# Two B loads of block 2 issued from GpSimd, and C of pairs 4 and 5 scaled ahead of their B

## The chip, the core and the metric

The kernel runs on one NeuronCore of a Trainium2 chip. The metric is the device time of one execution in microseconds (us). A core has five engines with a program each: TensorE (PE; its weight loads are shown as PEld), VectorE (DVE), ScalarE (ACT), GpSimd (POOL) and SyncE (SP). They wait for one another by semaphores. Loads and stores are issued by SyncE, ScalarE or GpSimd and carried out by 16 DMA engines.

## The reference

Two layers are computed one after the other. The first is a state-space recurrence in chunks (batch 4, 8 heads, 768 tokens, head size 32, state size 16):

```
cum = cumsum(log a) within the chunk;  L[i,j] = exp(cum[i]-cum[j]) for i >= j, else 0
y[i] = sum_j (C[i].B[j]) L[i,j] x[j]  +  (C[i].state) exp(cum[i])
state = exp(sum log a) state + sum_j B[j] x[j] exp(cum[last]-cum[j])
```

Its result, seen as 3072 tokens of 256 values, goes through a bilinear layer with d_ff = 1536: `out = ((y @ w_a) * (y @ w_b)) @ w_out`. Inputs and output are float32; the matrix products run on float16 operands.

## The kernel before

**Tiling.** The 768 tokens are cut into six blocks of 128. Blocks 0 and 1 and blocks 2 to 5 take somewhat different paths; the change is about block 2, the first that goes all the way by the later path. A *pair* is half of a block's scores: pairs 4 and 5 are heads 0 to 3 and heads 4 to 7 of block 2, each over all four batches. Decay is put on the operands: C is multiplied by running products of `a`, B by their inverses, so that the scores C.B need only the causal mask afterwards.

**The way of a pair from block 1 on.**
- *Loads.* `load_q` (L160) loads a block's C and B with eight DMAs of 64 KB, one for each of C and B and each batch, into two tiles, cq and bq (32 partitions for a batch). `ALL_Q` (L158) gives the order: C of batches 0 to 3, then B of batches 0 to 3. A tile thus serves both pairs of a block, and a pair needs all four batches. From block 2 on `loads_b` (L711) loads B of a pair a second time, by token, into bn, for the state sums; `loads_x` (L729) loads x from GpSimd.
- *Scaling.* `scale_q` (L341; the instruction is at L346) multiplies cq by FC, or bq by FB, into one of three float16 planes (pair 4 has plane 1, pair 5 plane 2), on GpSimd. FB is made by a reciprocal on VectorE (L309).
- *Turning.* `turn` (L353, instruction L359) transposes C and B of a plane with one VectorE instruction.
- *Scores.* `scores` (L398, L404): the matmuls of a pair (16 from block 2 on) into four PSUM banks.
- *Masks.* `mask` (L442): of the four score tiles of pairs 4 and 5, three on VectorE (L449); the fourth is copied out of PSUM by ScalarE (L446, into tmp) and masked by GpSimd (L447).
- *Output of a block.* `outputs` (L532): matmuls with the state (L536) and of scores and x (L473 or L485), the state sums (L501 or L512, from bn scaled into bm by GpSimd at L333), and ScalarE's copy into XB (L558). `state_spread` and `state_decay` (L576, L586) carry the state on, on GpSimd.

**The second layer.** `bunit` (L659) makes one of twelve k slices of a block: two matmuls for x @ w_a (aps), two for x @ w_b (bps, both L667), ScalarE's copy asb (L612), VectorE's product hkb (L679). `bout` (L685) multiplies with w_out (L693); ScalarE evacuates (L705), and the result is stored. Blocks 0 and 1 are stored later, from a list. The second layer of one block fills TensorE while the other engines prepare the pairs of the next.

**What sets the order.** It is written out by hand: the lines from L774 on are run with a manual schedule, and each engine executes its instructions in the order of these lines. A load is an instruction in the program of the engine that issues it. SyncE's and ScalarE's loads share eight completion semaphores in turn, and a load waits until the earlier one with its semaphore has landed; GpSimd's loads have eight of their own. Around the change:
- SyncE: x of pairs 2 and 3 (L819, four DMAs), B of pair 3 (L820, two), then block 2's eight loads (L888), bn of pairs 4 and 5 (L889), block 3's eight (L932), bn of pairs 6 and 7 (L941).
- GpSimd: C of pairs 2 and 3, B of pairs 2 and 3 (L871 to L874), Ge (L877), `spread(0)` with spair and gV (L883), the masks of pairs 2 and 3 (L899, L901, L913), bm of pairs 2 and 3 (L914, L915), causal_q (L916, L917), then C and B of pair 4 and C and B of pair 5 (L933, L934), x of pair 4 (L935), bm of pairs 4 and 5 (L940).
- VectorE: k slices 0 and 1 of block 1 (L946), turning of pair 4 (L947), slices 2 and 3 (L948). TensorE: the matmuls of these four slices, then the scores of pair 4 (L949).

Of the kernel before, what the change touches and what calls it, by code (L numbers as in the profile page):

```python
# [28 lines left out]
def kernel(  # L29
# [13 lines left out]
    nc = tc.nc  # L43
# [114 lines left out]
    ALL_Q = tuple((w, b) for w in (1, 0) for b in range(nb))  # L158

    def load_q(eng, blk, parts=ALL_Q):  # L160
        if blk not in by_batch:
            by_batch[blk] = [inq.tile([128, H, 4, N], f32, name=n_, tag=n_) for n_ in ("bq", "cq")]
        return [
            eng.dma_start(
                by_batch[blk][w][32 * b : 32 * b + 32].rearrange("i h s n -> i h (s n)"),
                (B, C)[w][b, :, blk * Q : (blk + 1) * Q, :].rearrange("h (i s) n -> i h (s n)", s=4),
            )
            for w, b in parts
        ]

    def load2(eng, p, which):
        if p < P2:
            return [load1(eng, p, which, bt) for bt in range(2)]
        blk, bp = divmod(p, NBP)
        src = (B, C, x)[which][2 * bp : 2 * bp + 2, :, blk * Q : (blk + 1) * Q, :]
        return [
            eng.dma_start(  # L177
                by_token(pair_in[p][which]).rearrange("p t h n -> p (t h) n"), src.rearrange("t h q n -> q (t h) n")
            )
        ]  # L180
# [160 lines left out]
    def scale_q(p, which, eng):  # L341
        blk, u = divmod(p, NBP)
        f = (FB, FC)[which][:, blk - PJ // NBP, :, 4 * u : 4 * u + 4].rearrange("p s j -> p j s")
        plane, step = planes[p % NR], (48, N)[which]
        c0 = (0, 192)[which]
        eng.tensor_tensor(  # L346
            out=plane[:, c0 : c0 + 4 * step].rearrange("p (j c) s -> p j s c", c=step)[:, :, :, 0:N],
            in0=by_batch[blk][which][:, 4 * u : 4 * u + 4],
            in1=f.unsqueeze(3).broadcast_to((128, 4, 4, N)),
            op=ALU.mult,  # L350
        )
# [359 lines left out]
    def loads_b(*ps):  # L711
        for p in ps:
            if p < NP:
                tiles(p)
                load2(nc.sync, p, 0)

    def loads_q(blk):
        if blk < NBLK:
            load_q(nc.sync, blk)
# [9 lines left out]
    def loads_x(p):  # L729
        if p < NP:  # L730
            load2(nc.gpsimd, p, 2)
# [5 lines left out]
    def prep(p):  # L737
        if p < NP:
            scale_q(p, 1, nc.gpsimd)
            scale_q(p, 0, nc.gpsimd)  # L740
# [144 lines left out]
    aps = [unit_mm(p, k2, Wa) for p, k2 in late]  # L885
    asb = [evac_a(a_ps) for a_ps in aps]
    load2(nc.scalar, 2, 0)
    load_q(nc.sync, 2)  # L888
    loads_b(4, 5)  # L889
    for (p, k2), a_sb_ in zip(late, asb):  # L890
        times(p, k2, unit_mm(p, k2, Wb), a_sb_)
# [36 lines left out]
    for c in range(3):  # L928
        p, bt = divmod(c, NBP)
        out_mm(p, bt, o[c], range(6, NK))  # L930
        out_store(p, bt, o[c])
    loads_q(3)  # L932
    prep(4)  # L933
    prep(5)  # L934
    loads_x(4)  # L935
    outputs(1)
    state_sums(1)
# [128 lines left out]
```

## Time and profile before

| | |
|---|---|
| time, three runs | median 123.27 us (122.97 to 123.49) |
| the profiled execution | 123.0 us, of which the span of the trace is 121.2 us |
| TensorE busy | 115.5 us, 95% of the span |
| VectorE, ScalarE, GpSimd busy | 90.1, 67.3 and 57.4 us |
| moved by DMA | 12.13 MB in 59777 packets |

The profile is that of one execution. A line of a timeline gives start and length in us from the start of the span, the engine, the line of the kernel, the operation, the tiles written and read, partitions x elements, and how many; in brackets stands the idle time of the engine ahead of it, and what ended it, inferred from semaphores. Where a wait has several semaphores, the name given may be of one that was not last. L12 is line 12 of the kernel before. "q" behind an engine (SPq) means its instruction queue: a load's length there is that of the issue, not of the transfer. Queue q1 is SyncE's, q10 ScalarE's, q0 GpSimd's; kind "instruction" is program code. Ends of matmuls are modelled.

### The profile page before, as it was taken

The page shows a single profiled execution, that of the slowest core. Times are in us where ns is not written, and L with a number is a line of the kernel's source. Part 1 is how long each engine was busy: PE and PEld are TensorE (multiplying, and loading weights), DVE is VectorE, ACT ScalarE, POOL GpSimd, SP SyncE. Part 2 cuts the span into 40 slices and gives each one's busy share as a digit, 9 for nine tenths or more (in the row PEclk, how much of TensorE's full clock was granted, in tenths as well). Part 3 has the DMA queues.
Part 4 walks back from the last instruction along what each step waited for, and adds up shares of the span by engine and source line. Part 5 has one row for each costly group of instructions (what it writes and reads, how often), then busy time and mean ns, then how long its engine had stood idle before and what let it go on. Part 6 is the DMA issues. An engine that isn't in the chain of part 4 may idle for free.

```text
span 121.2 us, 3574 instructions
## 1 busy us (share of the span) xinstructions
PE 115.5 (95%) x1399; PEld 75.4 (62%) x1400; DVE 90.1 (74%) x165; ACT 67.3 (56%) x133; POOL 57.4 (47%) x90
## 2 busy tenths in 40 slices
PE   7989999999979999999999999999999999999990
PEld 5546799888524478644476464766465684645880
DVE  4998989979969995599966999677889436748000
ACT  0446666696647654677655737535645637575220
POOL 7994989679179999396902995200000000000000
PEclk9999999999999999999999999999999999999998
DMA  3999999994679999979992909112001111010132
GB/s 63 133 182 192 208 234 190 202 155 94 93 105 108 123 117 151 109 103 125 238 186 87 86 2 124 10 46 92 0 0 46 32 43 60 0 43 0 49 108 65
DMA packets 59777, 12.13 MB, mean 100 GB/s; under 512 B 54992, under 2 KB 59728, under 8 KB 59760
## 3 DMA queue, kind: packets, MB, share of 16 engines
q0 software_dynamic: 20256, 3.67, 37.6%
q1 hardware_dynamic: 35920, 7.74, 34.0%
q10 hardware_dynamic: 3584, 0.49, 2.6%
q8 instruction: 11, 0.18, 0.7%
q14 instruction: 6, 0.05, 0.1%
HBM read 12.42 MB, written 3.15 MB: 128 GB/s over the span
## 4 chain that ended last, share of the span: by engine, by line
PE 91%; DVE 4%; issue 1%; ACT 1%; POOL 1%; ACTq 0%
PE ops L693 22%; PE aps L667 21%; PE bps L667 20%; PE ops L637 5%; PE aps L598 5%; PE bps L598 4%; PE SC L404 4%; PE SC L238 3%; PE SC L473 2%; DVE t L449 1%; PE SC L536 1%; PE py L458 1%; POOL planes L346 1%; PE tc L238 1%; PE SC L485 1%
## 5 line engine op out<-in xcount | busy, mean ns | idle before, releaser
L612 ACT COPY asb<-aps 128x512 f32<-128x512 f32 x72 | 41.9, 586 | 16.9 <-PE aps L667 13.3
L679 DVE TENSOR_TENSOR hkb<-bps,asb 128x512 f16<-128x512 f32 x60 | 40.2, 685 | 11.9 <-ACT asb L612 10.3
L667 PE MATMUL aps<-XB,Wa 128*128 128x512 f16 x120 | 35.8, 379 | 0.0
L667 PE MATMUL bps<-XB,Wb 128*128 128x512 f16 x120 | 35.7, 379 | 0.0
L693 PE MATMUL ops<-Wo,hkb 128*128 128x256 f16 (+1 forms) x252 | 28.1, 268 | 0.0
L693 PEld LDWEIGHTS <-hkb 128*128 128x128 f16 x252 | 23.0, 98 | 3.8
L667 PEld LDWEIGHTS <-Wb 128*128 128x128 f16 x120 | 12.4, 103 | 13.5
L667 PEld LDWEIGHTS <-Wa 128*128 128x128 f16 x120 | 12.1, 103 | 11.5 <-issue 0.2
L449 DVE TENSOR_TENSOR t<-SC,causal_q 128x512 f16<-128x512 f32 x27 | 17.3, 680 | 2.4 <-PE SC L404 2.4
L705 ACT ACTIVATE osb<-ops 128x256 f32<-128x256 f32 (+1 forms) x20 | 7.6, 378 | 18.4 <-PE ops L693 18.4
L447 POOL TENSOR_TENSOR t<-tmp,causal_q 128x512 f16<-128x512 f32 x5 | 5.8, 1158 | 8.8 <-ACT tmp L446 8.8
L177 POOL DMA_DIRECT2D xn<-in_x_dram x8 | 9.5, 1191 | 0.0
L346 POOL TENSOR_TENSOR planes<-bq,FB 128x256 f16<-128x256 f32 x10 | 7.5, 768 | 3.5 <-DVE hkb L679 3.4
L449 DVE TENSOR_TENSOR t<-SC,causal 128x512 f16<-128x512 f32 x11 | 6.9, 681 | 1.2 <-PE SC L404 1.1
L346 POOL TENSOR_TENSOR planes<-cq,FC 128x256 f16<-128x256 f32 x10 | 7.5, 771 | 0.1
L446 ACT COPY tmp<-SC 128x512 f32<-128x512 f32 x10 | 5.8, 588 | 2.9 <-PE SC L404 2.5
L622 DVE TENSOR_TENSOR hk<-bps,asb 128x512 f16<-128x512 f32 x11 | 7.2, 671 | 0.2 <-ACT asb L612 0.2
L558 ACT ACTIVATE XB<-SC 128x512 f16<-128x512 f32 (+1 forms) x9 | 4.6, 548 | 4.1 <-PE SC L501 2.4
L598 PE MATMUL aps<-X2T,Wa 128*128 128x256 f16 x48 | 6.8, 273 | 0.0
L598 PE MATMUL bps<-X2T,Wb 128*128 128x256 f16 x48 | 6.6, 272 | 0.0
L447 POOL TENSOR_TENSOR t<-tmp,causal 128x512 f16<-128x512 f32 x5 | 5.7, 1155 | 1.7 <-ACT tmp L446 1.6
L359 DVE STREAM_TRANSPOSE turned<-planes 128x384 f32<-128x384 f32 x10 | 5.5, 562 | 1.0 <-POOL planes L346 1.0
(100 smaller groups left out, 109.0 us busy)
## 6 DMA issues: line engine op xcount, KB each, us to landing
out_dram<-osb SPq DMA_DIRECT2D x23, 128.0 KB, 1.9
cq<-in_C_dram SPq DMA_DIRECT2D x20, 64.0 KB, 3.5
bq<-in_B_dram SPq DMA_DIRECT2D x20, 64.0 KB, 3.5
bn<-in_B_dram SPq DMA_DIRECT2D x8, 128.0 KB, 4.3
xn<-in_x_dram POOLq DMA_DIRECT2D x8, 128.0 KB, 5.4
Wa<-in_moe_w_a_dram POOLq DMA_DIRECT2D x2, 384.0 KB, 7.2
Wb<-in_moe_w_b_dram POOLq DMA_DIRECT2D x2, 384.0 KB, 7.7
Wo<-in_moe_w_out_dram POOLq DMA_DIRECT2D x2, 384.0 KB, 6.6
```

Source lines behind the costliest of these rows:

```text
L177: eng.dma_start(by_token(pair_in[p][which]).rearrange("p t h n -> p (t h) n"), src.rearrange("t h q n -> q (t h) n"))
L346: eng.tensor_tensor(out=plane[:, c0 : c0 + 4 * step].rearrange("p (j c) s -> p j s c", c=step)[:, :, :, 0:N], in0=by_batch[blk][which][:, ...
L447: nc.gpsimd.tensor_tensor(out=o_, in0=tmp, in1=c_, op=ALU.mult)
L449: nc.vector.tensor_tensor(out=o_, in0=i_, in1=c_, op=ALU.mult)
L598: nc.tensor.matmul(ps[:, kk * 2 * Q : (kk + 1) * 2 * Q], W[k // 6][:, f, k % 6 // 3 * 384 : (k % 6 // 3 + 1) * 384].rearrange("p (c kk) -> ...
L612: (nc.vector.tensor_copy if on_dve else nc.scalar.copy)(asb, a_ps)
L622: eng.tensor_tensor(out=s["hk"][:, 2 * k2 : 2 * k2 + 2, :].rearrange("p k q -> p (k q)"), in0=b_ps, in1=asb, op=ALU.mult)
L637: nc.tensor.matmul(o_ps[:, 0:d_model], hk[:, k, bt * Q : (bt + 1) * Q], Wo[:, k, :], start=(k == 0), stop=(k == NK - 1), skip_group_check= ...
L667: nc.tensor.matmul(t_, W[k // 6][:, f, k % 6 // 3 * 384 : (k % 6 // 3 + 1) * 384].rearrange("p (c kk) -> p kk c", kk=3)[:, k % 3], XB[:, b ...
L679: return lambda: nc.vector.tensor_tensor(out=s["hk"][:, k], in0=ps[1], in1=asb, op=ALU.mult)
L693: nc.tensor.matmul(o_ps[:, 0:w], hk[:, k, c * Q : (c + 1) * Q], Wo[:, k, cs], start=(k == 0), stop=(k == NK - 1), skip_group_check=True,)
L705: nc.scalar.activation(out=o_sb[:, 0:w], in_=o_ps[:, 0:w], func=AF.Copy, scale=1.0 / (YS * YS))
```

## The change

SyncE issues the first six of block 2's eight loads, C of four batches and B of batches 0 and 1. GpSimd issues B of batches 2 and 3, at the place in its program that follows gV and precedes the masks of pair 2. And GpSimd's four scalings for pairs 4 and 5 go in the order C of pair 4, C of pair 5, B of pair 4, B of pair 5. No instruction of TensorE, VectorE or ScalarE is added, removed or moved. Loads behind the two on SyncE's queue move up by two places, and so have other semaphores of the eight.

```diff
@@ -885,7 +885,8 @@
     aps = [unit_mm(p, k2, Wa) for p, k2 in late]
     asb = [evac_a(a_ps) for a_ps in aps]
     load2(nc.scalar, 2, 0)
-    load_q(nc.sync, 2)
+    load_q(nc.sync, 2, ALL_Q[:6])
+    load_q(nc.gpsimd, 2, ALL_Q[6:])
     loads_b(4, 5)
     for (p, k2), a_sb_ in zip(late, asb):
         times(p, k2, unit_mm(p, k2, Wb), a_sb_)
@@ -930,8 +931,9 @@
         out_mm(p, bt, o[c], range(6, NK))
         out_store(p, bt, o[c])
     loads_q(3)
-    prep(4)
-    prep(5)
+    for w in (1, 0):
+        for p in (4, 5):
+            scale_q(p, w, nc.gpsimd)
     loads_x(4)
     outputs(1)
     state_sums(1)
```

## Prediction

> **What bounds the kernel now.** I read the page first, then the chain that ended last, then the timelines of TensorE, GpSimd and SyncE around the one hole that the chain shows, then the landings of single loads. All quoted times are microseconds from the start of the span.
>
> ```profile
> PE 115.5 (95%) x1399; PEld 75.4 (62%) x1400; DVE 90.1 (74%) x165; ACT 67.3 (56%) x133; POOL 57.4 (47%) x90
> ...
> PE   7989999999979999999999999999999999999990
> ...
> PE 91%; DVE 4%; issue 1%; ACT 1%; POOL 1%; ACTq 0%
> ```
>
> TensorE is busy for 95% of the span and holds 91% of the chain. After the start there is one slice below 9 in its row, the twelfth (33.3 to 36.4), so only there can another engine's work be worth time. The chain in that stretch (start, length, what):
>
> ```profile
> 32.09 0.45 PE aps L667 x2
> ...
> 32.62 0.59 ACT asb L612
> ...
> 33.23 0.70 DVE hkb L679
> 33.94 0.19 issue
> 34.13 0.77 POOL planes L346
> ...
> 34.92 0.59 DVE turned L359
> ...
> 35.56 0.40 PE SC L404 x16
> ```
>
> The reader is to see the chain leave TensorE at 32.5 and come back at 35.56: GpSimd scales B of pair 4 into its plane, VectorE turns the plane, and the scores of pair 4 (L404) wait for that. What TensorE loses is seen in its own timeline (the bracket is idle time and what ended it):
>
> ```profile
> 33.66 0.59 PE L667 MATMUL aps<-XB,Wa 128*128 128x512 f16 x2
> 34.09 0.59 PE L667 MATMUL bps<-XB,Wb 128*128 128x512 f16 x2
> 35.56 0.40 PE L404 MATMUL SC<-turned 32*128 32x128 f16 x16 [0.87 <-DVE turned L359]
> ```
>
> Pairs of these matmuls follow each other every 0.43, so the scores could start at 34.09 + 0.43 = 34.52 and start at 35.56: the hole is **1.04**, of which the page counts 0.87 as idle because ends of matmuls are modelled. Why GpSimd was late:
>
> ```profile
> 22.65 0.62 POOL L586 TENSOR_TENSOR gV<-V,G 128x256 f32<-128x256 f32 x1
> 24.54 2.27 POOL L447 TENSOR_TENSOR t<-tmp,causal 128x512 f16<-128x512 f32 x2 [1.27 <-ACT tmp L446]
> 27.18 1.16 POOL L447 TENSOR_TENSOR t<-tmp,causal 128x512 f16<-128x512 f32 x1 [0.38 <-ACT tmp L446]
> ...
> 29.98 0.76 POOL L346 TENSOR_TENSOR planes<-cq,FC 128x256 f16<-128x256 f32 x1
> 34.13 0.76 POOL L346 TENSOR_TENSOR planes<-bq,FB 128x256 f16<-128x256 f32 x1 [3.38 <-DVE hkb L679]
> 34.73 0.77 POOL L346 TENSOR_TENSOR planes<-cq,FC 128x256 f16<-128x256 f32 x1
> ```
>
> The bracket names hkb, but the scaling of B reads neither hkb nor what it reads; it reads B of all four batches and FB. FB was made long before, so I look for a load. The second and the last of the four B loads of block 2, each asked for alone (durations in ns, start; then the time to landing):
>
> ```profile
> L164 SPq DMA_DIRECT2D bq<-in_B_dram x1: 449/449/449, 28.6 to 28.6; - x1
> ...
> DMA to landing us min/median/max: 2.4/2.4/2.4
> ```
>
> ```profile
> L164 SPq DMA_DIRECT2D bq<-in_B_dram x1: 449/449/449, 29.6 to 29.6; - x1
> ...
> DMA to landing us min/median/max: 4.0/4.0/4.0
> ```
>
> The second landed at 31.0; the last was issued at about 29.6 and landed at 33.6, and 0.55 later GpSimd began. So the cause is the last B load: issued late and slow to land. What made it slow stands in two windows of the DMA view, 31.2 to 32.6 and 32.7 to 33.7:
>
> ```profile
> q8 instruction: 1, 0.02, 4.6%
> ```
>
> ```profile
> q1 hardware_dynamic: 123, 0.01, 10.8%
> ```
>
> One packet of program code took 4.6% of 16 engines over 1.4, that is 1.0 of one engine. In the second window the load queue uses 10.8% of 16 engines, not quite two engines' worth, beside full use before. I read this as one DMA engine held up by the code packet and finishing alone.
>
> **The change part by part.** The queue of SyncE (start, length of all, count):
>
> ```profile
> 22.78 5.27 SPq L164 DMA_DIRECT2D cq<-in_C_dram  x4
> 28.09 1.93 SPq L164 DMA_DIRECT2D bq<-in_B_dram  x4
> 30.12 3.21 SPq L177 DMA_DIRECT2D bn<-in_B_dram  x2
> 33.38 2.47 SPq L164 DMA_DIRECT2D cq<-in_C_dram  x4
> ```
>
> *Two B loads leave SyncE.* Four take 1.93, or 0.49 each, so everything behind them (the two bn loads of pairs 4 and 5, then block 3) may go 0.98 earlier. The last B load on SyncE is now the second, issued at 28.6 and landing at 31.0 if nothing else moves.
>
> *Two B loads on GpSimd.* They stand behind gV, which ends at 22.65 + 0.62 = 23.27, ahead of the masks of pair 2. The trace has no load of this shape on GpSimd. Bounds from the nearest rows:
>
> ```profile
> 2.50 1.55 POOL L153 DMA_DIRECT2D xn<-in_x_dram  x2
> ```
>
> ```profile
> L177 POOL DMA_DIRECT2D xn<-in_x_dram x8 | 9.5, 1191 | 0.0
> ...
> xn<-in_x_dram POOLq DMA_DIRECT2D x4, 64.0 KB, 5.3
> Wb<-in_moe_w_b_dram POOLq DMA_DIRECT2D x2, 384.0 KB, 7.7
> ```
>
> Issuing costs 0.78 (the 64 KB loads by rows) to 1.19 (the 128 KB loads in short rows); I take 0.78, the same size. Two take 1.55 to 2.4 of a gap of 1.27, so the first two masks end 0.3 to 1.1 later than 26.81, at 27.1 to 27.9. The third began at 27.18: it moves by 0 to 0.7, and GpSimd's later wait of 3.38 takes that up. Cost on the path: 0. Landing takes 5.3 (same size) to 7.7 (six times the size): issued at 23.3 and 24.0, the loads are in by 29.4, or 31.7 at worst.
>
> *The transfers themselves.* 128 KiB come earlier, while the DMA engines still work on x of pairs 2 and 3, which SyncE issued last at 19.8. Its rows, and two stretches (columns: PE, PEld, DVE, ACT and POOL busy, clock, DMA share, GB/s):
>
> ```profile
> L153 SPq DMA_DIRECT2D x<-in_x_dram x1: 633/633/633, 19.8 to 19.8; - x1
> ...
> DMA to landing us min/median/max: 7.3/7.3/7.3
> ```
>
> ```profile
> 24.00:26.00 2.00, 2.00 (x34) 1.63 (x34) 1.70 (x3) 1.95 (x7) 1.46 (x2) 1.00 1.44 188
> ...
> 27.20:28.20 1.00, 1.00 (x11) 0.90 (x10) 1.00 (x2) 1.00 (x3) 1.00 (x1) 1.00 0.43 84
> ```
>
> The engines are full until about 27 and under half busy after. At 188 GB/s the two loads are worth 0.70, so the last x load, in at 27.1, slips by 0 (they only fill in) to 0.70 (all of it ahead); I take 0.4. SyncE's four C loads took 5.27 to issue where four B loads took 1.93: in the program a load there waits for the landing of an earlier one with the same semaphore, the fourth C load for the last x load. So the two remaining B loads slip too: the second is issued at 29.0 and lands at 31.4. The deadline is later: TensorE is ready at 34.52, the turning takes 0.59, the scaling 0.76, and the start came 0.55 after the landing, so a landing by 34.52 - 0.59 - 0.76 - 0.55 = 32.6 hides everything. The third B load, issued at about 29.1, still escaped the code packet; the fourth, at 29.6, did not. The margin is thus about 0.5 of further slip.
>
> *C of pair 5 ahead of B of pair 4.* It fills the wait: 29.98 + 0.60 (the pitch from 34.13 to 34.73) = 30.6. B of pair 4 then starts at 31.4 + 0.55 = 31.95 and is done by 32.7. Nothing but the deadline is left, and GpSimd has one scaling less behind it. If the landing came as late as before, the swap alone would gain nothing for pair 4.
>
> *What is late next.* VectorE runs in order, and its two hkb products end at 33.23 + 0.70 = 33.93. Turning then ends at 34.52 and the scores start at 34.52 to 34.6 instead of 35.56: **0.96 to 1.04, taken as 1.0**. After that:
>
> ```profile
> 35.50:45.00 9.50, 9.44 (x80) 5.27 (x81) 9.39 (x16) 6.01 (x11) 9.45 (x12) 1.00 1.52 119
> ```
>
> TensorE is busy for 9.44 of 9.50, so a start that is 1.0 earlier goes through to the end, if VectorE (9.39) and GpSimd (9.45) follow. Both do: VectorE sat idle from 33.93 to 34.92 for the same plane and starts 1.0 earlier, GpSimd starts over 2 earlier. The two bn loads are issued about 0.6 earlier (0.98 less the slip), ahead of their need.
>
> The sum: span 121.2 - 1.0 = 120.2. The profiled execution took 123.0, 0.27 under the median of 123.27; by the same difference it becomes 122.0, and the median 123.27 - 1.0 = **122.3**.
>
> **The rivals.** *The gain is given back in the DMA engines.* If x slips by 0.9 or more, the second B load goes out where the fourth did, meets the code packet and lands at about 33.6: no gain, 123.3; in between, at a landing of 33.2, 0.4 is left and the time is 122.9. For it: the engines are full when GpSimd issues. Against it: 0.70 is the upper bound by the row. The Trainium skill, "DMA: Bandwidth & Descriptors", section "Issuing engines are not separate DMA queues", speaks for this rival: loads from all engines share the same 16 DMA engines, and another issuer saves only the issue time. The trace agrees that the engines are shared (a DMA share over 1 while GpSimd's weights and SyncE's loads both move); that only issue time counts is not what the row of the fourth B load shows, which lost 1.6 by being behind.
>
> *GpSimd's own loads land late*, after 32.6, which needs 8.6 from issue where the rows show 5.3 and 7.7. Then 122.6 to 123.3.
>
> *VectorE gives the second half back*: at 9.39 of 9.50 any new disturbance there stalls TensorE. Half lost: 122.8.
>
> *Slower: x comes too late for block 1.* The last x is cast on ScalarE and read by TensorE:
>
> ```profile
> 27.00 1.14 ACT L725 CAST xn<-x 128x512 f16<-128x512 f32 x2
> ```
>
> ```profile
> 29.34 0.77 PE L485 MATMUL SC<-t,xn 64*32 64x128 f16 x61
> ```
>
> The second cast ends at 28.14 and is needed at 29.34: a slip beyond 1.2 is paid one to one, and the B loads are then late as well. At a slip of 2.1, three times the estimate, 0.9 is lost: 124.2. It decides from 1.2 on; over 1.8 it can be measured. A GpSimd transfer that costs the engines three times its bytes would do it, and no row of this shape excludes that.
>
> The change not doing what it says would need GpSimd to issue late; nothing ahead of the two loads waits for more than it did, so that gets no chance of its own.
>
> **How the numbers follow.** The forecast (0.65 or more gained): 0.70. Given back in the DMA engines: 0.13; GpSimd's loads late: 0.04; VectorE: 0.05; slower: 0.08. A measurement of this kernel can tell about 0.5%, or 0.62, from no change. So faster 0.70, the same 0.22 (the three middle cases), slower 0.08. The range: the lowest run shown, 122.97, less 1.04 and some 0.1 for the reading of the trace gives 121.8; upwards it takes in the VectorE case and the upper half of the first rival, to 123.1. Left out are the slower case, the loads that gain nothing, in all about 0.19.
>
> **What would show it.** In the new profile the idle time ahead of L404 at about 34.5 is gone or under 0.2; B of pair 4 is scaled at about 32 and the turning follows hkb without a gap; the two GpSimd loads are issued at 23.3 to 24.8 and land before 30; SyncE's second B load is issued between 28.6 and 29.3; the masks of pair 2 slip by 0.3. A landing of that second load after 33, a cast of x after 29, or a new hole in TensorE's row behind 36 would make the prediction wrong.

## The result, and the profile after

The changed kernel takes 122.30 us (median of 21 runs) against 122.97 us for the kernel before (21 runs on the same chips); the ratio is **0.9957, 95% interval 0.9937 to 0.9976**. That is 0.53 us faster (0.30 to 0.77, the interval times 122.97). The ratio is that of the means and leaves out one slow run of the changed kernel (123.83 us), so it says less than the 0.67 between the medians. "No change" lies outside the interval, but the gain lies within the 0.5% that the prediction set as the bound of what can be told. The profiled execution took 122.13 us, its span is 120.4 us.

The page of the changed kernel, the same rows as before:

```profile
PE 115.9 (96%) x1399; PEld 75.6 (63%) x1400; DVE 90.1 (75%) x165; ACT 67.4 (56%) x133; POOL 58.9 (49%) x92
...
PE   7999999999999999999999999999999999999990
...
PE 92%; DMA 2%; DVE 2%; ACT 1%; issue 0%
```

The twelfth slice, which was 7, is 9. The chain in that stretch (start, length, what):

```profile
33.87 0.43 PE aps L667 x2
34.30 0.43 PE bps L667 x2
34.73 0.33 PE SC L404 x16
35.07 0.55 PE aps L667 x2
```

Where the chain left TensorE for ScalarE, VectorE and GpSimd, it now stays on TensorE. TensorE's timeline shows the scores of pair 4 with no idle time ahead of them:

```profile
34.14 0.59 PE L667 MATMUL bps<-XB,Wb 128*128 128x512 f16 x2
34.67 0.40 PE L404 MATMUL SC<-turned 32*128 32x128 f16 x16
```

They start 0.53 after the last pair of matmuls began; in the trace of before it was 35.56 - 34.09 = 1.47. The difference, 0.94, is what the hole cost there. GpSimd's timeline of the changed kernel tells how it was filled:

```profile
23.31 1.22 POOL L164 DMA_DIRECT2D bq<-in_B_dram  x2
24.59 2.27 POOL L447 TENSOR_TENSOR t<-tmp,causal 128x512 f16<-128x512 f32 x2
27.24 1.16 POOL L447 TENSOR_TENSOR t<-tmp,causal 128x512 f16<-128x512 f32 x1 [0.37 <-ACT tmp L446]
...
29.28 0.62 POOL L333 TENSOR_TENSOR bm<-bn,fB 128x256 f16<-128x256 f32 x1 [0.30 <-DMA bn<-in_B_dram]
...
30.70 1.37 POOL L346 TENSOR_TENSOR planes<-cq,FC 128x256 f16<-128x256 f32 x2 [0.29 <-DMA cq<-in_C_dram]
31.90 1.37 POOL L346 TENSOR_TENSOR planes<-bq,FB 128x256 f16<-128x256 f32 x2
```

The reader is to see two things. The wait of 3.38 ahead of B of pair 4 is gone: B is scaled at 31.90 instead of 34.13, right behind the two C scalings. And two short waits are new, 0.30 for bn and 0.29 for cq: loads on SyncE's queue that land later than in the trace of before. (In two more traces of the changed kernel, below, the wait for cq is there once and the one for bn not at all.) VectorE's timeline has the turning of pair 4 directly behind hkb:

```profile
32.53 1.44 DVE L679 TENSOR_TENSOR hkb<-bps,asb 128x512 f16<-128x512 f32 x2
33.89 0.57 DVE L359 STREAM_TRANSPOSE turned<-planes 128x384 f32<-128x384 f32 x1
```

### The profile page after: what moved, and what is told of

Same layout as the page of the kernel before. It is cut to its first block, busy times and chain, and to the rows that moved or that the text cites. A ratio compares the mean times of both kernels' runs of the same rounds, so it can differ in the third digit from the quotient of the medians.

```text
span 120.4 us, 3575 instructions
## 1 busy us (share of the span) xinstructions
PE 115.9 (96%) x1399; PEld 75.6 (63%) x1400; DVE 90.1 (75%) x165; ACT 67.4 (56%) x133; POOL 58.9 (49%) x92
## 4 chain that ended last, share of the span: by engine, by line
PE 92%; DMA 2%; DVE 2%; ACT 1%; issue 0%
PE ops L693 23%; PE aps L667 22%; PE bps L667 22%; PE aps L598 5%; PE ops L637 5%; PE bps L598 4%; PE SC L404 4%; DMA a_sb<-in_a_dram 2%; PE SC L473 2%; DVE t L449 1%; PE SC L238 1%; PE SC L536 1%; PE py L458 1%; PE tc L238 1%; PE SC L485 1%; PE fps L271 1%
## 5 line engine op out<-in xcount | busy, mean ns | idle before, releaser
L238 PE MATMUL SC<-const-bfloat16-1.0 128*128 128x256 bf16 (+2 forms) x24 | 5.2, 382 | 0.8 <-PEq L1052 0.8
```

Source lines behind the costliest of these rows:

```text
L238: nc.tensor.matmul(bank[:, 0:cols], nc.const_aps.tensor(1.0, [128, 128], mybir.dt.bfloat16), nc.const_aps.tensor(1.0, [128, cols], mybir.d ...
```

## The experiments

The ratios of the first four experiments are to 27 runs of the kernel before (median 123.06 us).

**One half alone: the loads.** Only the first hunk of the diff:

```diff
-    load_q(nc.sync, 2)
+    load_q(nc.sync, 2, ALL_Q[:6])
+    load_q(nc.gpsimd, 2, ALL_Q[6:])
```

> Only the two B loads go to GpSimd; the scaling order stays C4, B4, C5, B5. Theory (the last B load on SyncE landed too late, and taking two loads off its queue cures that): B of pair 4 is scaled at 31.3 to 31.6, the turning follows hkb at about 33.9 without a gap, no idle time ahead of L404 at 34.7, ratio to the kernel before 0.993 to 0.998, the same as with both edits. Rival (the gain comes from C of pair 5 filling GpSimd's wait): little or no gain, 0.998 to 1.002.

Measured: 0.9962 (0.9933 to 0.9991), median 122.45. GpSimd and TensorE in its trace:

```profile
31.05 0.77 POOL L346 TENSOR_TENSOR planes<-cq,FC 128x256 f16<-128x256 f32 x1 [0.32 <-DMA cq<-in_C_dram]
31.65 0.78 POOL L346 TENSOR_TENSOR planes<-bq,FB 128x256 f16<-128x256 f32 x1
```

```profile
34.45 0.59 PE L667 MATMUL bps<-XB,Wb 128*128 128x512 f16 x2
34.98 0.40 PE L404 MATMUL SC<-turned 32*128 32x128 f16 x16
```

No hole, and the time of the whole change within the intervals. B of pair 4 was scaled at 31.65, at the edge of the 31.3 to 31.6 expected, with all of this execution 0.3 later. The last B loads had landed by then, GpSimd's at 29.9 and SyncE's at 31.3. The theory holds: the loads alone make the gain.

**The other half alone: the order of scaling.** Only the second hunk:

```diff
-    prep(4)
-    prep(5)
+    for w in (1, 0):
+        for p in (4, 5):
+            scale_q(p, w, nc.gpsimd)
```

> Only the scaling order changes; all eight loads stay on SyncE. Theory: B of pair 4 still waits for the last B load and is scaled at 33 to 34.2, the hole ahead of L404 stays (0.4 to 1.0), GpSimd's later work is 0.6 earlier without use, ratio 0.998 to 1.002. Rival (the order makes the gain): ratio 0.993 to 0.998.

Measured: 1.0004 (0.9965 to 1.0042), median 123.22. Its trace:

```profile
30.32 1.36 POOL L346 TENSOR_TENSOR planes<-cq,FC 128x256 f16<-128x256 f32 x2
34.35 1.37 POOL L346 TENSOR_TENSOR planes<-bq,FB 128x256 f16<-128x256 f32 x2 [2.67 <-DVE hkb L679]
```

```profile
35.78 0.40 PE L404 MATMUL SC<-turned 32*128 32x128 f16 x16 [0.76 <-DVE turned L359]
```

C of pair 5 shortens GpSimd's wait from 3.38 to 2.67 and changes nothing for who waits behind it: B of pair 4 is scaled when the last B load has landed (at 34.35, a little after the 33 to 34.2 expected). The time alone would not settle it, since the interval reaches down to 0.9965 and the rival's range up to 0.998; the wait in the trace speaks against the rival.

**The same relief of SyncE, a later issue.** The changed kernel, with GpSimd's two loads moved behind bm of pair 3:

```diff
-    load_q(nc.gpsimd, 2, ALL_Q[6:])
     loads_b(4, 5)
...
     scale_bc(3, 0, nc.gpsimd)
+    load_q(nc.gpsimd, 2, ALL_Q[6:])
```

> As the changed kernel, but GpSimd issues the two B loads behind bm of pair 3, at about 29.9 and 30.5, and no longer in the gap at 23.3; SyncE's queue is relieved just the same. Theory (when the last B lands is what counts, and the early place is what GpSimd's queue gives): they land 4 to 5.5 after issue, 34 to 36, B of pair 4 is scaled at 34.5 to 36.5, the hole ahead of L404 is 1.3 to 3.3 long, ratio 1.003 to 1.02. Rival (what counts is the issue time saved on SyncE): as the changed kernel, 0.994 to 0.998.

Measured: 1.0084 (1.0052 to 1.0116), median 123.94. Its trace:

```profile
29.97 1.22 POOL L164 DMA_DIRECT2D bq<-in_B_dram  x2
...
35.32 1.36 POOL L346 TENSOR_TENSOR planes<-bq,FB 128x256 f16<-128x256 f32 x2 [2.21 <-DMA bq<-in_B_dram]
```

```profile
36.74 0.40 PE L404 MATMUL SC<-turned 32*128 32x128 f16 x16 [1.53 <-DVE turned L359]
```

SyncE issues just as little as in the changed kernel, and the kernel is slower than before. What counts is when the last B lands, and it lands early only because GpSimd's program reaches the loads early. All figures fell within the theory's bounds.

**Why the last B load was late: short rows or program code?** The kernel before, with bn of pairs 4 and 5 issued behind block 3's loads:

```diff
-    loads_b(4, 5)
     for (p, k2), a_sb_ in zip(late, asb):
...
     loads_q(3)
+    loads_b(4, 5)
     prep(4)
```

> The kernel before, with the bn loads of pairs 4 and 5 issued behind block 3's loads, so that no short rows follow the last B load. If the packet of program code alone makes the last B load late, it ends its engine's share at about 32.5 to 32.9 (the code packet's end) and the hole shrinks to 0.1 to 0.4; if the bn rows behind it also matter, the landing is earlier than the 33.6 of before by 0.7 to 1.8; if neither matters, it lands at 33.6 as before and the hole stays at 0.9. bn lands at 38 to 41, so bm of pairs 4 and 5 and what stands behind it on GpSimd may be 2 late; the time itself may go either way, 0.99 to 1.02.

Measured: 1.0177 (1.0107 to 1.0248), from two runs only. The last B load, asked for alone, then two windows of the DMA view (31.6 to 32.8 and 32.8 to 33.6), then TensorE:

```profile
L164 SPq DMA_DIRECT2D bq<-in_B_dram x1: 453/453/453, 29.6 to 29.6; - x1
...
DMA to landing us min/median/max: 4.4/4.4/4.4
```

```profile
q8 instruction: 1, 0.02, 5.8%
```

```profile
q1 hardware_dynamic: 57, 0.01, 11.8%
```

```profile
35.94 0.40 PE L404 MATMUL SC<-turned 32*128 32x128 f16 x16 [1.06 <-DVE turned L359]
```

With no bn rows behind it the last B load still took 4.4 and landed at 34.0, so the short rows are not the cause. Again a packet of code took 1.1 of one engine (5.8% of 16 over 1.2; a packet is counted in whole in the window in which it starts), and afterwards under two engines' worth (11.8% of 16) worked off 57 packets. But the code packet alone had been priced at a landing of 32.5 to 32.9, and that was 1 short. What came is nearest to the third case that was set down, in which neither the packet nor the rows matter. So this run rules out the short rows and does not show that the packet is the cause; the table of landings further down speaks to that. The longer time is the price of the late bn loads (from the scores of pair 4 to the end it is 84.6, where it is 82.8 in the kernel before), seen in GpSimd's timeline and then in TensorE's:

```profile
38.58 0.62 POOL L333 TENSOR_TENSOR bm<-bn,fBl 128x256 f16<-128x256 f32 x1 [1.10 <-DMA bn<-in_B_dram]
41.16 0.62 POOL L333 TENSOR_TENSOR bm<-bn,fBl 128x256 f16<-128x256 f32 x1 [1.97 <-DMA bn<-in_B_dram]
```

```profile
47.95 0.46 PE L473 MATMUL SC<-t,xn 128*32 128x128 f16 x20 [1.05 <-DMA xn<-in_x_dram]
48.82 0.24 PE L473 MATMUL SC<-t,xn 128*32 128x128 f16 x4 [0.41 <-POOL t L447]
```

GpSimd stood waiting for bn, so the x load and the mask behind it on its queue were late, and TensorE waited for both.

**How often is the hole there?** The kernel before again, in three more profiled executions, to see whether the hole in the one trace was typical. The expectations call each such execution a look; below they are repeats.

> The kernel before once more, unchanged, for its trace alone. Theory of the size (the hole of 1.04 in the one trace is a draw from many: how late the last B load lands depends on whether and when a DMA engine is held by the code packet, so the mean hole is near 0.5): over the looks the landing of the last B load and the hole ahead of L404 vary together, from 0 to over 1, and the time of a look is the shorter the smaller the hole. Rival (the hole is always about 1.0, and the change loses 0.4 elsewhere): the hole is 0.85 to 1.05 in each look.

> As the first look at the kernel before: theory, a hole between 0 and 1.1 that follows the landing of the last B load; rival, 0.85 to 1.05 again.

> As the first look at the kernel before: theory, a hole between 0 and 1.1 that follows the landing of the last B load; rival, 0.85 to 1.05 again.

Two more at the kernel before, and two at the changed kernel:

> The kernel before, unchanged, for its trace. So far its four traces had a hole ahead of L404 three times (0.79 to 0.94 idle) and none once. Theory (the hole is there in most executions, not all): 0.7 to 1.0 or none. Rival: some value in between as often.

> As the fourth look at the kernel before: a hole of 0.7 to 1.0, or none.

> The changed kernel once more, for its trace. Theory: B of pair 4 is scaled before 32.5 and there is no idle time ahead of L404, and the span differs from the other trace by what the first 31 us differ alone (the rest from the scores of pair 4 on takes 82.8). Rival (the loads on GpSimd land late in some executions): a hole here too.

> As the second look at the changed kernel: no hole ahead of L404; rival, a hole in some.

In each trace I take the start of the first matmul of k slice 0 of block 1 and the start of the scores of pair 4. Repeat 1, no hole; repeat 2, a hole:

```profile
31.66 0.59 PE L667 MATMUL aps<-XB,Wa 128*128 128x512 f16 x2
...
35.21 0.40 PE L404 MATMUL SC<-turned 32*128 32x128 f16 x16
```

```profile
31.00 0.59 PE L667 MATMUL aps<-XB,Wa 128*128 128x512 f16 x2
...
35.55 0.40 PE L404 MATMUL SC<-turned 32*128 32x128 f16 x16 [0.94 <-DVE turned L359]
```

| trace | first matmul | scores of pair 4 | between |
|---|---|---|---|
| before, the first | 31.07 | 35.56 | 4.49 |
| before, repeat 1 | 31.66 | 35.21 | 3.55 |
| before, repeat 2 | 31.00 | 35.55 | 4.55 |
| before, repeat 3 | 30.93 | 35.33 | 4.40 |
| before, repeat 4 | 31.39 | 35.89 | 4.50 |
| before, repeat 5 | 31.75 | 35.30 | 3.55 |
| changed, the first | 31.12 | 34.67 | 3.55 |
| changed, repeat 2 | 31.26 | 34.81 | 3.55 |
| changed, repeat 3 | 31.71 | 35.26 | 3.55 |

So 3.55 is the time without a hole. The changed kernel has it in all three traces, the kernel before in two of six; in the other four the hole is 0.85 to 1.00. The mean of the six is 0.62. From the scores of pair 4 to the end of the last instruction it is 82.8 in every one of the nine. What remains of the spread is in the first 31 us (30.93 to 31.75 for the first matmul), in both kernels. The theory of the size holds, in the sharper form written ahead of the last repeats: the hole is there nearly whole or not at all. One of its expectations failed: the time of an execution does not follow the hole alone, since repeats 1 and 5, without a hole, had the latest starts.

Where there was no hole, the last B load was not caught. In repeat 5 it was in before the code packet came (31.7 by the rows below; the second fence is the window 31.7 to 32.7):

```profile
L164 SPq DMA_DIRECT2D bq<-in_B_dram x1: 448/448/448, 29.4 to 29.4; - x1
...
DMA to landing us min/median/max: 2.3/2.3/2.3
```

```profile
q8 instruction: 1, 0.02, 7.1%
```

In repeat 1 a code packet came in the window 31.0 to 31.7:

```profile
q8 instruction: 1, 0.02, 14.2%
```

It took 1.6 of one engine (14.2% of 16 over 0.7), and B, issued at 29.5, still landed at 31.8.

Narrower windows give the start of each packet. And a trace records the landing of a load as sixteen updates of its semaphore, as many as there are DMA engines; the view prints only the last. I read each update as the share of one engine, and call it a part. For the last B load on SyncE, in all eight traces in which SyncE issues it fourth:

| trace | code packet starts | first part in | fifteenth | sixteenth | hole |
|---|---|---|---|---|---|
| before, the first | 31.45 | 31.38 | 31.96 | 33.58 | 0.94 |
| before, repeat 1 | 31.02 | 31.13 | 31.56 | 31.82 | none |
| before, repeat 2 | 31.36 | 31.10 | 32.42 | 33.55 | 1.00 |
| before, repeat 3 | 31.13 | 30.71 | 32.36 | 33.33 | 0.85 |
| before, repeat 4 | 31.68 | 31.31 | 32.99 | 33.88 | 0.95 |
| before, repeat 5 | 31.95 | 31.13 | 31.58 | 31.67 | none |
| order of scaling alone | 31.63 | 31.32 | 32.90 | 33.80 | 0.83 |
| bn late | 31.64 | 31.32 | 33.01 | 33.95 | 1.14 |

In the six traces with a hole the packet starts while the parts are landing, and one part comes 0.9 to 1.6 behind the fifteenth, 1.1 to 1.2 after the packet's end. In the two without, the packet starts ahead of the first part (by 0.1) or behind the last. This is what one engine held by the packet would look like, and it fits all eight; still, the profile does not name the DMA engine of a packet, and no run moved one. Why the part takes 1.1 more after the packet, and why in five of the six the fifteenth part is late too (32.4 to 33.0), stays open. The packet itself starts 0.2 to 0.5 after the first matmul of k slice 0 in twelve of the thirteen traces of the kernels so far (repeat 1 is the exception), so a late start of TensorE brings a late packet. In the changed kernel's three traces SyncE's last B load is in 0.5 to 0.8 ahead of it.

**Another second issuer.** The changed kernel with ScalarE in GpSimd's place:

```diff
-    load_q(nc.gpsimd, 2, ALL_Q[6:])
+    load_q(nc.scalar, 2, ALL_Q[6:])
```

> As the changed kernel, but ScalarE issues the two B loads, at the same place in the program lines. ScalarE's loads share the eight semaphores with SyncE's, so the first waits for the landing of a bn load of pair 3 (about 28.0) and the second for one of pair 2 (27.4), and ScalarE's copies behind them wait too. Theory (it is GpSimd's own semaphores and its idle gap that make the early issue free): ScalarE stands still from about 21 to 28, TensorE starves for lack of PSUM banks, the time is 3 to 7 longer, ratio 1.025 to 1.06. Rival (any second issuer does): as the changed kernel, 0.994 to 0.998.

Measured in one execution: 129.8 us, where a run of the kernel before beside it took 122.27, so 7.5 longer. ScalarE's queue and what waited behind it:

```profile
25.54 2.25 ACTq L164 DMA_DIRECT2D bq<-in_B_dram  x2
27.89 1.07 ACT L612 COPY asb<-aps 128x512 f32<-128x512 f32 x2 [7.70 <-DMA bq<-in_B_dram]
```

```profile
28.53 1.01 PE L598 MATMUL aps<-X2T,Wa 128*128 128x256 f16 x4 [5.99 <-ACT asb L612]
```

The mechanism is the expected one, a little dearer than its upper bound: the two loads were issued at 25.5 and 27.5, as semaphores shared with SyncE came free (those of two x loads, and not of bn loads as expected); until then ScalarE's copies waited, 7.7 in all, and TensorE 6.0.

## Why the prediction was right, and where a size was off

*The cause of the hole.* Right for the wait: it ends with the last B load on SyncE. That a packet of code on one DMA engine makes it late fits the landings in all eight traces of the table, and the fourth experiment rules out the short rows; no run moved a packet, so this step is borne out by coincidence in time and not by an edit. The Trainium skill, "Runtime: NRT & Kernel Launch", section "Instruction fetch mechanics", says that an engine's instruction memory is refilled in blocks of 16 KiB, which are 256 instructions. The trace agrees in number: the page of the profile lists 11 packets of 0.18 MB in all on queue q8, 16 KB each, and TensorE's 1399 matmuls and 1400 weight loads are 10.9 times 256.

*Two loads leave SyncE.* Right in kind, and earlier than forecast: the second B load was issued at 28.4 and landed 2.5 later, at 30.9 (forecast 29.0 and 31.4). The third experiment shows that the relief by itself is not the gain.

*Two loads on GpSimd.* Issuing took 1.22 (forecast 1.55) and fits the gap of 1.27; the masks did not slip. Landing took 5.6 and 5.5 by their rows (forecast 5.3):

```profile
L164 POOL DMA_DIRECT2D bq<-in_B_dram x1: 632/632/632, 23.3 to 23.3; - x1
...
DMA to landing us min/median/max: 5.6/5.6/5.6
```

*The slip of other loads.* The last x load was to slip by 0.4; in the first trace it landed 7.2 after 20.0, at 27.2, where it was 27.1. The last bn load of pair 3 and the last C load were later instead. The bn load, asked for alone (before, then changed):

```profile
L153 SPq DMA_DIRECT2D bn<-in_B_dram x1: 997/997/997, 21.7 to 21.7; - x1
...
DMA to landing us min/median/max: 6.2/6.2/6.2
```

```profile
L153 SPq DMA_DIRECT2D bn<-in_B_dram x1: 2364/2364/2364, 21.7 to 21.7; - x1
...
DMA to landing us min/median/max: 7.5/7.5/7.5
```

bn of pair 3 landed 1.3 later and the last C load 0.9 later (27.2 + 3.4 after 27.2 + 2.5). These are the two new waits on GpSimd. But one trace of each kernel cannot tell a slip from scatter. Over the six traces of the kernel before and the three of the changed one, the last x load lands at 26.3 to 27.5 (mean 27.1) and 27.2 to 27.6 (27.4), the bn load at 27.8 to 28.9 (28.2) and 28.4 to 29.2 (28.8), the last C load at 29.3 to 30.3 (29.7) and 30.3 to 30.6 (30.5). So C is late by about 0.8; x by 0.3, near the forecast, and bn by 0.6 are within what the executions differ. bm of pair 3 at 29.28 was still ahead of TensorE, and C was needed only to keep B of pair 4 before the deadline, so nothing was lost.

*C of pair 5 first.* Right that it would gain nothing by itself; it gains nothing measurable beside the loads either (0.9962 without it, 0.9957 with it).

*What is late next, and the rest.* Turning was forecast at 33.93 and began at 33.89; the scores were forecast at 34.52 to 34.6 and began at 34.67, because they follow the last pair of matmuls by 0.53 and not by 0.43. That makes the hole 0.94 instead of 1.04. The gain goes through to the end undiminished (82.8 in all nine traces), so the rival in which VectorE gives half back has fallen.

*The step that was mis-sized* is the sum itself, 1.0 off the median: it took the hole of the one trace for the hole of every execution. Its mean over six traces is 0.62, and 0.53 (0.30 to 0.77) was measured. The predicted time of 122.3 agrees with the measured 122.30 partly by chance: the kernel before has a median of 122.97 over 21 runs, not 123.27 over three, and the gain is smaller by about as much. So the mechanism is the forecast's, but its case, 0.65 or more gained, was missed by a little (the interval still takes it in), and by its own bound the result is the upper end of "the same".

*The rivals.* That the gain is given back in the DMA engines did not happen. Of the two sentences of the Trainium skill named there, the one that the engines are shared agrees with the C load that lands 0.8 later, the one that only issue time is saved is not: the third experiment saves SyncE the same issue time and loses 0.84%. GpSimd's loads landed at 28.9 and 29.4 with over 3 to spare. The slower case needed x to slip by 1.2; in none of the three traces did it land over 0.5 later than the 27.1 of the forecast's trace.

## What to carry to other kernels

When a wait ends with the last of several loads, look at each load's own landing: here three of four were in by 31.2 and the last at 33.6, and the cure was to issue early from a queue that was free then, not to fill the wait. A second issuer helped here only where its program reached the loads early and it shared no semaphores with the first. And a stall that comes from a collision is in some executions and not in others: look at several traces before pricing it at its size in one.

## What the runs showed of the hardware that was not expected

A 16 KB packet of program code took 1.0 to 1.1 us of one DMA engine in the six traces with a hole, and a 64 KB load in flight with it took 4.0 to 4.4 us to land, where it took 2.3 in the two traces in which the packet did not start while the parts of the load landed; when the packet starts differs from run to run. A 64 KB load of 256 rows took GpSimd only 0.6 us to issue, less than the 0.78 of the loads of x, which the page also counts at 64 KB but which have 512 rows by the kernel's `load1`. And after TensorE had stood still for 6 us (ScalarE issuing), its granted clock was half for a while (columns: PE, PEld, DVE, ACT and POOL busy, clock, DMA share, GB/s):

```profile
22.50:28.50 6.00, 0.04 (x1) 0.00 (x0) 0.00 (x0) 0.61 (x2) 1.28 (x3) 0.71 1.06 165
28.50:31.00 2.50, 2.47 (x36) 1.67 (x39) 2.23 (x4) 1.05 (x2) 0.00 (x0) 0.50 0.58 131
31.00:40.00 9.00, 9.00 (x214) 7.01 (x207) 7.27 (x14) 6.59 (x17) 7.17 (x11) 0.95 0.77 110
```

At half clock for 2.5 and at 0.95 for 9, about 1.7 is lost by estimate (1.25 and 0.45), 7.7 with the 6.0 in which TensorE stood still. That fits: its k slice 0 of block 1 begins at 38.91, where it begins at 31.12 to 31.71 in the three traces of the changed kernel.
